# Ten V slots, wq tails that share partitions, softmax sums in place, and new output projection rates

## The chip, the cores and the metric

The kernel runs on one core of a Trainium2 chip. The time is the device time of one execution in microseconds (us); the profile is one execution taken by the hardware profiler. The engines are TensorE (PE; PEld is its weight load), VectorE (DVE), ScalarE (ACT), GpSimd (POOL) and SyncE (SP), which issues nearly all transfers here.

## What is computed

Two independent attention blocks, A and B, with shapes that are the same: 16 batches, 144 query rows of width 448, 16 heads of width 256, 512 cached keys, all in bf16. The two outputs are set side by side.

```python
def _A_ref(x, k_cache, v_cache, wq, wo):          # _B_ref is the same, with rep = 1
    B, Sq, D = x.shape                            # 16, 144, 448
    H, Dh = 16, 256
    q = (x @ wq).reshape(B, Sq, H, Dh).transpose(0, 2, 1, 3)
    scores = jnp.einsum("bhqd,bhkd->bhqk", q, k_cache) * (Dh ** -0.5)
    p = softmax(scores, axis=-1)
    o = jnp.einsum("bhqk,bhkd->bhqd", p, v_cache)
    return o.transpose(0, 2, 1, 3).reshape(B, Sq, H * Dh) @ wo
```

## The kernel before, in words

A **unit** is one head of one batch: 512 units, A's in 0 to 255, B's in 256 to 511 (the first 32 alternate between batches 0 and 1, the rest go batch by batch). For each unit the kernel makes the query `q` (transposed, from `wq` and `x`), the scores against K (transposed, keys on the partitions), the exponentials, and the product with V; four slices of 128 keys each. The result is scaled by the reciprocal of the row sums and put into `ring`, three chunks of 128 output rows long, from which the output projection takes it. A chunk's projection is 32 pieces (one matrix product of 128 x 448 each, `t_op_piece`, L1335), issued in twos; there are 18 chunks for each block.

**The order of the work** is written out by a loop over steps `i` (L1515 on). Step `i` issues, in this order: transfers whose step has come, a query product for unit i+3 or i+4 with its cast (`t_q`, `t_evac_q`), the scores of unit i+2 or i+3 with their exponentials (`t_s`, L1163 and L1173), the V product of unit i (`t_pv`, L1219), the product that makes the row sums (`t_sum`, L1235), the fold of unit i+2 (`t_halves`, L1197), the two adds of unit i+3 on POOL (`t_presum`, L1183 and L1188), logarithm and reciprocal of the sums on ScalarE (`t_ln`, `t_recip`), two checks of the sums' size (`t_check`), the scaling into `ring` (`t_evac_ot`, L1271), and pieces of the output projection. Each engine executes its list in that order and waits by semaphores; a small bookkeeper (`_Sched`) derives the waits from what each instruction reads and writes, tile by tile.

**The row sums.** POOL adds the exponentials of slices 0, 1 to those of 2, 3 (`pp_sb`), then the two halves of that to each other. From unit 48 on (`P0`) that second add goes to `p2_sb`, and VectorE folds its upper 64 partitions onto the lower ones into half of `ps_sb` (one half for an even unit, one for the odd one after it), so that one matrix product with blocks of ones makes the sums of two units. `ln` goes to `ln_sb`, and two exponentials of 64 partitions each make the reciprocal in one of two slots of `rinv_sb`.

**The queries.** `x` has 448 columns: three slices of 128 and a tail of 64. `wq_sb` holds four slices; in the fourth, partitions 64 to 127 are zero, so that whatever `x`'s fourth slice has there doesn't count. From unit 48 on one query product serves the same head of two neighbouring batches where it can (288 columns in place of 144), every second step.

**Transfers.** A planner in Python (L1414 to L1510) lays all loads in one order for SyncE: each load has a use (a step), a step from which its place is free, and an assumed duration. V comes in pairs of units into a ring of `NV` = 9 slots, in which the first 48 units' K also lies (those are transposed by TensorE); later K comes 16 units at a time by a transposing transfer (`t_load_k`, L1039) into a ring for 32 units. `wq` and `wo` of B take the place of A's while the kernel goes over from A to B.

**The rate of the projection.** `op_schedule` (L1378) gives a credit at each step: `OP_RATE` times 18 x 32 / 256 pieces. Its entries are (up to this unit, rate). Pieces that are ready and have credit go into that step. In the last 30 steps the credit is raised, so that all that is ready goes out.

Of the kernel before, what the change touches and what calls it, by code (L numbers as in the profile page):

```python
# [752 lines left out]
def bass_concat_heads__mha_block_cached__gqa_block_cached__near_ridge_kernel(  # L753
# [41 lines left out]
    NV, NX = 9, 6  # L795
# [7 lines left out]
    NQT, NPT, NPS, NRI, NOST = 11, 4, 2, 2, 2  # L803
# [3 lines left out]
    OP_DELAY, OP_START, OP_RATE = 2, (28, 16), ((240, 1.0), (292, 1.35), (600, 1.15))  # L807
# [5 lines left out]
    NRUN = max(n for n in range(1, 33) if NCK % n == 0)  # L813
# [9 lines left out]
    with contextlib.ExitStack() as es:  # L823
# [8 lines left out]
        wq_sb = sb("wq_sb", [128, 4, H * DH], BF16)  # L832
# [4 lines left out]
        xt_sb = sb("xt_sb", [128, 4, NX, SQ], BF16)  # L837
        qt_sb = sb("qt_sb", [128, NQT, 2, SQ], BF16)
# [3 lines left out]
        ps_sb = sb("ps_sb", [128, NPS, SQ], BF16)  # L842
        rinv_sb = sb("rinv_sb", [128, NRI, SQ], F32)
        p2_sb = sb("p2_sb", [128, SQ], F32)
        ln_sb = sb("ln_sb", [128, SQ], F32)
        run_sb = sb("run_sb", [128, 2, NRUN], BF16)
        runs_sb = sb("runs_sb", [128, 2, NCK // NRUN], F32)
        ost_sb = sb("ost_sb", [128, NOST, D], BF16)
        stat = sb("stat", [128, 4], F32)
        flag_sb = sb("flag_sb", [128, 4], I32)  # L850
# [52 lines left out]
        def t_init():  # L903
# [10 lines left out]
            def e2(v):  # L914
                return v.memset(wq_sb[64:128, 3, :], 0.0)
            S.add(DVE, e2, writes=[("wqz", 0)], name="wqz")
# [21 lines left out]
        def t_load_wq(pr, h0, h1, eng=SP):  # L938
            cols = slice(h0 * DH, h1 * DH)
            w = wqs[pr]  # L940
            sem = "wq%d" % (h0 // 4 if h1 != 1 and h1 != 2 else HG + h0)

            def e(q):
                q.dma_start(wq_sb[:, 0:3, cols], w[0:384, cols].rearrange("(c p) n -> p c n", p=128)).then_inc(
                    sems[sem], 16)
                return q.dma_start(wq_sb[0:64, 3, cols], w[384:448, cols]).then_inc(sems[sem], 16)
            S.add(eng, e, writes=[(("wq", h), pr) for h in range(h0, h1)], dma_sem=sem, n_dma=2,
                  name="wq%d.%d" % (pr, h0))
# [59 lines left out]
        def t_tr_x(g):  # L1008
# [19 lines left out]
            S.add(ACT, e2, reads=[("opp", ("x", g))], writes=[(("xt", g), g)], banks=["op"], name="exa%d" % g)  # L1028

# [90 lines left out]
        def t_q(U):  # L1120
# [5 lines left out]
            def e(t):  # L1126
                ins = None
                for dc in range(2):
                    for kc in range(4):
                        c0 = h * DH + dc * 128  # L1130
                        acc = qp_ps[:, dc, 0:2 * SQ] if n == 2 else qp_ps[:, 0, dc * SQ:(dc + 1) * SQ]
                        ins = t.matmul(acc, lhsT=wq_sb[:, kc, c0:c0 + 128],  # L1132
                                       rhs=xt_sb[:, kc, xo:xe + 1:max(xe - xo, 1), :], start=(kc == 0), stop=(kc == 3))
                return ins
            S.add(PE, e, reads=[(("wq", h), pr), ("wqz", 0)] + [(("xt", g % NX), g) for g in gs],
# [41 lines left out]

        def t_presum(U):
            psl = U % NPT
            sl = U % NPS  # L1180
# [4 lines left out]
            dst, key = (ps_sb[:, sl, :], (("ps", sl), U)) if U < P0 else (p2_sb[:, :], ("p2", U))  # L1185
# [5 lines left out]
        def t_halves(U):  # L1191

            sl = U // 2 % NPS
            p0 = U % 2 * 64

            def e(v):
                return v.tensor_tensor(ps_sb[p0:p0 + 64, sl, :], p2_sb[0:64, :], p2_sb[64:128, :], op=ALU.add)  # L1197

            S.add(DVE, e, reads=[("p2", U)], writes=[(("ps", sl), ("p", U // 2)), ("halves", U)], name="hv%d" % U)
# [26 lines left out]
        def t_sum(U):  # L1226
            ob = U % 2
            if U < P0:
                rhs, keys = ps_sb[:, U % NPS, :], [("ones", 0), (("ps", U % NPS), U)]
            else:  # L1230
                sl = U // 2 % NPS
                rhs, keys = ps_sb[:, sl, :], [("ones", 1), (("ps", sl), ("p", U // 2))]
# [5 lines left out]
        def t_ln(U):  # L1238
            ob = U % 2
            dst, key = (rinv_sb[:, U % NRI, :], (("rinv", U % NRI), (U, 0))) if U < P0 else (ln_sb[:, :], ("ln", U))  # L1240
# [5 lines left out]
        def t_recip(U):  # L1246
# [6 lines left out]
            h0 = U % 2 * 64  # L1253
            for p0 in (0, 64):
                def e(a, p0=p0):
                    return a.activation(rinv_sb[p0:p0 + 64, sl, :], ln_sb[h0:h0 + 64, :], AF.Exp, scale=-1.0)  # L1256
# [395 lines left out]
```

## Time and profile before

| | |
|---|---|
| median of 7 runs | 1047.29 us (1045.80 to 1053.54) |
| profiled execution | 1049.42 us, its span 1047.70 us |
| granted TensorE clock, mean | 0.997 |
| bytes moved by DMA | 294.1 MB, mean 281 GB/s |
| V loads | 256 of 512 KB, median 7.5 to 7.7 us from issue to landing |
| K loads by transposing transfers | 30, median 23.1 us (A) and 25.2 us (B) to landing |

A line of the page's groups reads: line of the kernel, engine, operation, what it writes <- what it reads, shape, count | busy us, mean ns of one | idle time of the engine just before it, and what ended it. In a timeline a line is: start, duration, engine, line, operation; instructions of one kind in a row are merged, and a number in brackets is the engine's idle time before it. A row of windows has the stretch, its length, busy time (and count) of PE, PEld, DVE, ACT and POOL, the granted clock, the DMA share and GB/s. A row of waits has who waited for whom: us in total, times, longest.

### The profile page before, as it was taken

The page shows a single profiled execution, that of the slowest core. Times are in us where ns is not written, and L with a number is a line of the kernel's source. Part 1 is how long each engine was busy: PE and PEld are TensorE (multiplying, and loading weights), DVE is VectorE, ACT ScalarE, POOL GpSimd, SP SyncE. Part 2 cuts the span into 40 slices and gives each one's busy share as a digit, 9 for nine tenths or more (in the row PEclk, how much of TensorE's full clock was granted, in tenths as well). Part 3 has the DMA queues.
Part 4 walks back from the last instruction along what each step waited for, and adds up shares of the span by engine and source line. Part 5 has one row for each costly group of instructions (what it writes and reads, how often), then busy time and mean ns, then how long its engine had stood idle before and what let it go on. Part 6 is the DMA issues. An engine that isn't in the chain of part 4 may idle for free.

```text
span 1047.7 us, 32447 instructions
## 1 busy us (share of the span) xinstructions
PE 1031.8 (98%) x12432; PEld 876.1 (84%) x12432; DVE 742.2 (71%) x2042; ACT 794.3 (76%) x2368; POOL 636.8 (61%) x1030
## 2 busy tenths in 40 slices
PE   8999999999999999999999899999999999999997
PEld 8999888888888888888887788888888888888885
DVE  5776677777677776777776567777776667777775
ACT  5877678778777777778766668787877777788785
POOL 3654556666666666666655556666665656666673
PEclk9999999999999999999999999999999999999999
DMA  9999999999999999999999999999999999999960
GB/s 319 360 347 323 294 277 273 279 275 277 303 280 323 260 266 253 278 305 294 257 284 338 279 280 294 290 282 304 267 282 265 294 265 316 266 276 286 289 216 13
DMA packets 590884, 294.10 MB, mean 281 GB/s; under 512 B 501440, under 2 KB 515904, under 8 KB 590720
## 3 DMA queue, kind: packets, MB, share of 16 engines
q1 hardware_dynamic: 590240, 291.72, 111.7%
q8 instruction: 99, 1.62, 0.6%
q14 instruction: 65, 0.53, 0.1%
q10 hardware_dynamic: 480, 0.23, 0.1%
HBM read 161.74 MB, written 4.13 MB: 158 GB/s over the span
## 4 chain that ended last, share of the span: by engine, by line
PE 93%; DMA 4%; ACT 1%; DVE 1%; SPq 1%; issue 0%; POOL 0%; ACTq 0%; DVEq 0%
PE s_ps L1163 23%; PE qp_ps L1132 23%; PE ot_ps L1219 23%; PE op_ps L1335 19%; DMA kt_sb<-in_B_k_cache_dram 2%; PE ot_ps L1235 2%; PE s_ps L1083 1%; PE qp_ps L1083 1%; PE qp_ps L1335 1%; DMA wq_sb<-in_B_wq_dram 1%; DMA v_sb<-in_B_v_cache_dram 1%; ACT rinv_sb L1256 0%; DMA v_sb<-in_A_k_cache_dram 0%; ACT pt_sb L1173 0%; SPq L1053 0%
## 5 line engine op out<-in xcount | busy, mean ns | idle before, releaser
L1183 POOL TENSOR_TENSOR pp_sb<-pt_sb 128x288 f32<-128x288 bf16 x512 | 385.0, 752 | 314.8 <-ACT pt_sb L1173 299.9
L1173 ACT ACTIVATE pt_sb<-s_ps 128x288 bf16<-128x288 f32 x1024 | 364.5, 408 | 178.8 <-PE s_ps L1163 172.6
L1271 DVE TENSOR_TENSOR ring<-ot_ps,rinv_sb 128x288 bf16<-128x288 f32 (+2 forms) x640 | 242.0, 395 | 149.8 <-ACT rinv_sb L1256 146.3
L1163 PE MATMUL s_ps<-qt_sb,kt_sb 128*128 128x144 bf16 x4096 | 340.6, 226 | 3.8 <-DMA kt_sb<-in_B_k_cache_dram 3.0
L1219 PE MATMUL ot_ps<-pt_sb,v_sb 128*128 128x144 bf16 x4096 | 339.9, 226 | 1.6 <-DMA v_sb<-in_B_v_cache_dram 1.6
L1163 PEld LDWEIGHTS s_ps<-qt_sb,kt_sb 128*128 128x128 bf16 x4096 | 287.3, 98 | 56.8 <-DVE qt_sb L1146 6.4
L1256 ACT ACTIVATE rinv_sb<-ln_sb 64x144 f32<-64x144 f32 x928 | 298.3, 321 | 24.2
L1132 PE MATMUL qp_ps<-xt_sb,wq_sb 128*128 128x288 bf16 (+1 forms) x2368 | 301.1, 270 | 2.7 <-DVE kt_sb L1091 1.5
L1335 PE MATMUL op_ps<-wo_sb,ring 128*128 128x448 bf16 x1120 | 285.6, 353 | 0.0
L1132 PEld LDWEIGHTS qp_ps<-xt_sb,wq_sb 128*128 128x128 bf16 x2368 | 211.1, 98 | 77.9 <-DVE kt_sb L1091 1.6
L1219 PEld LDWEIGHTS ot_ps<-pt_sb,v_sb 128*128 128x128 bf16 x4096 | 274.0, 98 | 2.5 <-DMA v_sb<-in_B_v_cache_dram 1.8
L1188 POOL TENSOR_TENSOR p_sb<-pp_sb 128x144 f32<-128x144 f32 x464 | 227.5, 490 | 75.0 <-DVE ps_sb L1197 10.7
L1286 DVE TENSOR_REDUCE run_sb<-ot_ps 128x1 bf16<-128x144 f32 x560 | 146.6, 304 | 77.4 <-ACT ln_sb L1243 45.0
L1197 DVE TENSOR_TENSOR ps_sb<-p_sb 64x144 bf16<-64x144 f32 x464 | 159.9, 345 | 45.6 <-POOL p_sb L1188 31.7
L1146 DVE CAST qt_sb<-qp_ps 128x576 bf16<-128x576 f32 x216 | 162.1, 750 | 17.2 <-PE qp_ps L1132 14.6
L1335 PEld LDWEIGHTS op_ps<-wo_sb,ring 128*128 128x128 bf16 x1120 | 93.7, 98 | 20.1
L1243 ACT ACTIVATE ln_sb<-ot_ps 128x144 f32<-128x144 f32 x232 | 67.9, 293 | 33.7 <-PE ot_ps L1235 26.9
L1235 PE MATMUL ot_ps<-ps_sb,ones 128*128 128x144 bf16 x280 | 63.3, 226 | 0.0
L1145 DVE CAST qt_sb<-qp_ps 128x288 bf16<-128x288 f32 x80 | 35.9, 449 | 2.0 <-PE qp_ps L1132 1.5
L1091 ACT ACTIVATE kt_sb<-qp_ps 128x512 bf16<-128x512 bf16 x48 | 28.9, 602 | 1.2 <-PE qp_ps L1083 1.2
L1188 POOL TENSOR_TENSOR ps_sb<-pp_sb 128x144 bf16<-128x144 f32 x48 | 23.5, 490 | 6.9 <-PE ot_ps L1235 0.3
L1235 PEld LDWEIGHTS ot_ps<-ps_sb,ones 128*128 128x128 bf16 x280 | 27.4, 98 | 0.0
(37 smaller groups left out, 162.5 us busy)
## 6 DMA issues: line engine op xcount, KB each, us to landing
v_sb<-in_A_v_cache_dram SPq DMA_DIRECT2D x128, 512.0 KB, 7.7
v_sb<-in_B_v_cache_dram SPq DMA_DIRECT2D x128, 512.0 KB, 7.5
v_sb<-in_A_k_cache_dram SPq DMA_DIRECT2D x22, 512.0 KB, 10.0
out_dram<-ost_sb SPq DMA_DIRECT2D x36, 112.0 KB, 6.9
wo_sb<-in_A_wo_dram SPq DMA_DIRECT2D x8, 448.0 KB, 7.9
wo_sb<-in_B_wo_dram SPq DMA_DIRECT2D x8, 448.0 KB, 8.6
wq_sb<-in_B_wq_dram SPq DMA_DIRECT2D x4, 768.0 KB, 10.0
wq_sb<-in_A_wq_dram SPq DMA_DIRECT2D x3, 768.0 KB, 9.3
```

What stands on the lines that cost most here:

```text
L1132: ins = t.matmul(acc, lhsT=wq_sb[:, kc, c0:c0 + 128], rhs=xt_sb[:, kc, xo:xe + 1:max(xe - xo, 1), :], start=(kc == 0), stop=(kc == 3))
L1146: return v.tensor_copy(qt_sb[:, a:b + 1:b - a, :, :], qp_ps[:, :, 0:2 * SQ].rearrange("p e (u q) -> p u e q", u=2))
L1163: ins = t.matmul(s_ps[bank][:, (c % 2) * SQ:(c % 2 + 1) * SQ], lhsT=kt_sb[:, 2 * c + dc, ko:ko + 128], rhs=qt_sb[:, qsl, dc, :], start=(dc ...
L1173: return a.activation(pt_sb[:, psl, 2 * k:2 * k + 2, :].rearrange("p b q -> p (b q)"), s_ps[bank][:, 0:2 * SQ], AF.Exp, scale=DH ** -0.5)
L1183: return g.tensor_tensor(pp_sb[:, :, :], pt_sb[:, psl, 0:2, :], pt_sb[:, psl, 2:4, :], op=ALU.add)
L1188: return g.tensor_tensor(dst, pp_sb[:, 0, :], pp_sb[:, 1, :], op=ALU.add)
L1197: return v.tensor_tensor(ps_sb[p0:p0 + 64, sl, :], p2_sb[0:64, :], p2_sb[64:128, :], op=ALU.add)
L1219: ins = t.matmul(ot_ps[ob][:, dc * SQ:(dc + 1) * SQ], lhsT=v_sb[:, vsl, j, c * DH + dc * 128:c * DH + (dc + 1) * 128], rhs=pt_sb[:, sl, c, ...
L1256: return a.activation(rinv_sb[p0:p0 + 64, sl, :], ln_sb[h0:h0 + 64, :], AF.Exp, scale=-1.0)
L1271: ins = v.tensor_tensor(ring[:, 2 * h:2 * h + 2, r0:r0 + q1 - q0], ot_ps[ob][:, 0:2 * SQ].rearrange("p (c q) -> p c q", c=2)[:, :, q0:q1], ...
L1286: return v.tensor_reduce(run_sb[:, k, j:j + 1], ot_ps[ob][:, 2 * SQ:3 * SQ], axis=AX.X, op=op)
L1335: ins = t.matmul(acc[0:m, 0:D], lhsT=ring[:, c, col0:col0 + m], rhs=wo_sb[:, c, :], start=(c == op_first), stop=(c == op_last))
```

## The change

It does six things.

- **A tenth V slot** (`NV` = 10). The planner's rules stay; with ten slots its answer differs.
- **wq's tail shared by two heads.** `wq_sb` has three slices; the tails (64 rows) lie in `wqt_sb`, the even head's in partitions 0 to 63, the odd head's in 64 to 127. A load of wq then has one transfer for the three slices and two for the tails, in runs of 512 bytes. An even head's fourth product reads `xt_sb`'s fourth slice, an odd one's `xu_sb`. So `x`'s tail has to be copied to partitions 64 to 127 of `xu_sb`, and partitions 64 to 127 of `xt_sb`'s fourth slice have to be zero: `t_tail_x`, on VectorE, a copy and a memset for each batch, two or three steps before the batch's first query. The loads of x are planned for three steps earlier.
- **Sums in place.** `p2_sb` goes: the second add writes `pp_sb`'s first half. `ps_sb` has one slot in place of two; before unit 48 odd units use a part of `ost_sb`.
- **Logarithm in place.** `ln_sb` goes: `ln` is written to the odd unit's reciprocal slot; the reciprocal of the odd unit is made in place.
- **Small stores**: `runs_sb` in bf16, `flag_sb` inside `stat`, the checks' runs 20 long in place of 28.
- **Rates**: 1.04 up to unit 200, 0.85 to 240, 1.4 to 292, then 1.1; before 1.0 to 240, 1.35 to 292, then 1.15.

```diff
-    NV, NX = 9, 6
+    NV, NX = 10, 6
...
-    NQT, NPT, NPS, NRI, NOST = 11, 4, 2, 2, 2
+    NQT, NPT, NRI, NOST = 11, 4, 2, 2
...
-    OP_DELAY, OP_START, OP_RATE = 2, (28, 16), ((240, 1.0), (292, 1.35), (600, 1.15))
+    OP_DELAY, OP_START, OP_RATE = 2, (28, 16), ((200, 1.04), (240, 0.85), (292, 1.4), (600, 1.1))
...
-    NRUN = max(n for n in range(1, 33) if NCK % n == 0)
+    NRUN = max(n for n in range(1, 21) if NCK % n == 0)
...
-        wq_sb = sb("wq_sb", [128, 4, H * DH], BF16)
+        wq_sb = sb("wq_sb", [128, 3, H * DH], BF16)
+        wqt_sb = sb("wqt_sb", [128, H // 2 * DH], BF16)
...
+        xu_sb = sb("xu_sb", [128, NX, SQ], BF16)
...
-        ps_sb = sb("ps_sb", [128, NPS, SQ], BF16)
+        ps_sb = sb("ps_sb", [128, SQ], BF16)
...
-        p2_sb = sb("p2_sb", [128, SQ], F32)
-        ln_sb = sb("ln_sb", [128, SQ], F32)
...
-        runs_sb = sb("runs_sb", [128, 2, NCK // NRUN], F32)
+        runs_sb = sb("runs_sb", [128, 2, NCK // NRUN], BF16)
...
-        stat = sb("stat", [128, 4], F32)
-        flag_sb = sb("flag_sb", [128, 4], I32)
+        stat = sb("stat", [128, 8], F32)
+        flag_sb = stat.bitcast(I32)[:, 4:8]
...
-                return v.memset(wq_sb[64:128, 3, :], 0.0)
-            S.add(DVE, e2, writes=[("wqz", 0)], name="wqz")
+                return v.memset(xu_sb[0:64, :, :], 0.0)
+            S.add(DVE, e2, writes=[("xuz", 0)], name="xuz")
...
+            p0, p1 = h0 // 2, (h1 + 1) // 2
+            tails = [] if h0 % 2 else [0, 1]
+
...
-                q.dma_start(wq_sb[:, 0:3, cols], w[0:384, cols].rearrange("(c p) n -> p c n", p=128)).then_inc(
+                ins = q.dma_start(wq_sb[:, 0:3, cols], w[0:384, cols].rearrange("(c p) n -> p c n", p=128)).then_inc(
...
-                return q.dma_start(wq_sb[0:64, 3, cols], w[384:448, cols]).then_inc(sems[sem], 16)
-            S.add(eng, e, writes=[(("wq", h), pr) for h in range(h0, h1)], dma_sem=sem, n_dma=2,
-                  name="wq%d.%d" % (pr, h0))
+                for k in tails:
+                    src = w[384:448, p0 * 2 * DH:p1 * 2 * DH].rearrange("p (g e n) -> p g e n", e=2, n=DH)[:, :, k, :]
+                    dst = wqt_sb[k * 64:k * 64 + 64, p0 * DH:p1 * DH].rearrange("p (g n) -> p g n", n=DH)
+                    ins = q.dma_start(dst, src).then_inc(sems[sem], 16)
+                return ins
+            S.add(eng, e, writes=[(("wq", h), pr) for h in range(h0, h1)] + [(("wqt", p), pr) for p in range(p0, p1) if tails],
+                  dma_sem=sem, n_dma=1 + len(tails), name="wq%d.%d" % (pr, h0))
...
+        def t_tail_x(g):
+            sl = g % NX
+
+            def e1(v):
+                return v.tensor_copy(xu_sb[64:128, sl, :], xt_sb[0:64, 3, sl, :])
+            S.add(DVE, e1, reads=[(("xt", sl), g)], writes=[(("xu", sl), g)], name="xu%d" % g)
+            if g in X_AT:
+                return
+
+            def e2(v):
+                return v.memset(xt_sb[64:128, 3, sl, :], 0.0)
+            S.add(DVE, e2, reads=[(("xt", sl), g)], writes=[(("xt", sl), g)], name="xz%d" % g)
+
...
-                        ins = t.matmul(acc, lhsT=wq_sb[:, kc, c0:c0 + 128],
-                                       rhs=xt_sb[:, kc, xo:xe + 1:max(xe - xo, 1), :], start=(kc == 0), stop=(kc == 3))
+                        w, x = wq_sb[:, kc, c0:c0 + 128] if kc < 3 else wqt_sb[:, h // 2 * DH + dc * 128:][:, 0:128], xt_sb[:, kc]
+                        if kc == 3 and h % 2:
+                            x = xu_sb
+                        ins = t.matmul(acc, lhsT=w, rhs=x[:, xo:xe + 1:max(xe - xo, 1), :], start=(kc == 0), stop=(kc == 3))
...
-            S.add(PE, e, reads=[(("wq", h), pr), ("wqz", 0)] + [(("xt", g % NX), g) for g in gs],
+            S.add(PE, e, reads=[(("wq", h), pr), (("wqt", h // 2), pr), ("xuz", 0)] + [(("xt", g % NX), g) for g in gs] +
+                  ([(("xu", g % NX), g) for g in gs] if h % 2 else []),
...
+        def ps_natural(U):
+            if U % 2:
+                return ost_sb[:, 1, 0:SQ], (("ost", 1), ("ps", U))
+            return ps_sb[:, :], ("ps", U)
+
...
-            sl = U % NPS
...
-            dst, key = (ps_sb[:, sl, :], (("ps", sl), U)) if U < P0 else (p2_sb[:, :], ("p2", U))
+            dst, key = ps_natural(U) if U < P0 else (pp_sb[:, 0, :], ("pp", ("p2", U)))
...
-            sl = U // 2 % NPS
...
-                return v.tensor_tensor(ps_sb[p0:p0 + 64, sl, :], p2_sb[0:64, :], p2_sb[64:128, :], op=ALU.add)
-
-            S.add(DVE, e, reads=[("p2", U)], writes=[(("ps", sl), ("p", U // 2)), ("halves", U)], name="hv%d" % U)
+                return v.tensor_tensor(ps_sb[p0:p0 + 64, :], pp_sb[0:64, 0, :], pp_sb[64:128, 0, :], op=ALU.add)
+
+            S.add(DVE, e, reads=[("pp", ("p2", U))], writes=[("ps", ("p", U // 2)), ("halves", U)], name="hv%d" % U)
...
-                rhs, keys = ps_sb[:, U % NPS, :], [("ones", 0), (("ps", U % NPS), U)]
+                rhs, key = ps_natural(U)
+                keys = [("ones", 0), key]
...
-                sl = U // 2 % NPS
-                rhs, keys = ps_sb[:, sl, :], [("ones", 1), (("ps", sl), ("p", U // 2))]
+                rhs, keys = ps_sb[:, :], [("ones", 1), ("ps", ("p", U // 2))]
...
-            dst, key = (rinv_sb[:, U % NRI, :], (("rinv", U % NRI), (U, 0))) if U < P0 else (ln_sb[:, :], ("ln", U))
+            sl = U % NRI if U < P0 else NRI - 1
+            dst, key = rinv_sb[:, sl, :], (("rinv", sl), (U, 0))
...
-            h0 = U % 2 * 64
-            for p0 in (0, 64):
-                def e(a, p0=p0):
-                    return a.activation(rinv_sb[p0:p0 + 64, sl, :], ln_sb[h0:h0 + 64, :], AF.Exp, scale=-1.0)
-                S.add(ACT, e, reads=[("ln", U // 2 * 2)], writes=[(("rinv", sl), U)], name="rc%d.%d" % (U, p0))
+            if U % 2 == 0:
+                for p0 in (0, 64):
+                    def e(a, p0=p0):
+                        return a.activation(rinv_sb[p0:p0 + 64, 0, :], rinv_sb[0:64, NRI - 1, :], AF.Exp, scale=-1.0)
+                    S.add(ACT, e, reads=[(("rinv", NRI - 1), (U, 0))], writes=[(("rinv", 0), U)], name="rc%d.%d" % (U, p0))
+                return
+
+            def e(a):
+                a.activation(rinv_sb[0:64, NRI - 1, :], rinv_sb[64:128, NRI - 1, :], AF.Exp, scale=-1.0)
+                return a.activation(rinv_sb[64:128, NRI - 1, :], rinv_sb[64:128, NRI - 1, :], AF.Exp, scale=-1.0)
+            S.add(ACT, e, writes=[(("rinv", NRI - 1), U)], name="rc%d" % U)
...
-                load(first_q[g0], (g1 - NX) * H - lq(NT) if g1 > NX else s_min, 1.3 + 0.55 * (g1 - g0), t_load_x, XG)
+                load(first_q[g0] - 3, (g1 - NX) * H - lq(NT) if g1 > NX else s_min, 1.3 + 0.55 * (g1 - g0), t_load_x, XG)
...
+            for g, at_q in first_q.items():
+                if (-2 + g if g in X_AT else at_q - 2 - g % 2) == i:
+                    t_tail_x(g)
```

## The prediction

> **What bounds the kernel now.** I read the page's first two parts, then the chain that ended last, the waits of TensorE, windows over the stages, SyncE's issues, and timelines of single steps.
>
> ```profile
> PE 1031.8 (98%) x12432; PEld 876.1 (84%) x12432; DVE 742.2 (71%) x2042; ACT 794.3 (76%) x2368; POOL 636.8 (61%) x1030
> ...
> PE 93%; DMA 4%; ACT 1%; DVE 1%; SPq 1%; issue 0%; POOL 0%; ACTq 0%; DVEq 0%
> ```
>
> TensorE is busy for 1031.8 of 1047.7 us and is 93% of the chain. The change takes no matrix product away: a query's fourth slice still has 128 rows, half of them zeros on one side. So it can only win back TensorE's waits, or add some.
>
> ```profile
> PE s_ps L1163 <- DMA kt_sb<-in_B_k_cache_dram: 3.0, 1, 3.0
> PE ot_ps L1219 <- DMA v_sb<-in_B_v_cache_dram: 1.6, 1, 1.6
> PE qp_ps L1132 <- DVE kt_sb L1091: 1.5, 1, 1.5
> ...
> PE qp_ps L1132 <- DMA wq_sb<-in_B_wq_dram: 0.9, 1, 0.9
> ```
>
> Three of these lie at the passage from problem A to B: at 521.5 us (wq of B), 561.6 (V) and 600.5 (K). Together 5.5 us, and the last also costs clock:
>
> ```profile
> 601.75:605.20 3.45, 3.45 (x22) 2.60 (x20) 1.52 (x3) 1.12 (x4) 1.15 (x2) 0.51 1.04 387
> 605.20:608.00 2.80, 2.80 (x33) 2.20 (x31) 1.46 (x6) 2.31 (x8) 1.63 (x3) 1.00 1.07 405
> ```
>
> The third number from the right is the granted clock: about half for 3.4 us, so some 1.7 us lost. The passage holds 5.5 + 1.7 = **7.2 us** that a better order of transfers could win. The other side is how closely the softmax sums run, seen in the last units (start, duration):
>
> ```profile
> 1022.67 0.30 DVE L1197 TENSOR_TENSOR ps_sb<-p_sb 64x144 bf16<-64x144 f32 x1
> 1022.78 0.79 POOL L1183 TENSOR_TENSOR pp_sb<-pt_sb 128x288 f32<-128x288 bf16 x1
> ...
> 1024.03 0.45 DVE L1145 CAST qt_sb<-qp_ps 128x288 bf16<-128x288 f32 x1
> 1024.49 0.73 POOL L1183 TENSOR_TENSOR pp_sb<-pt_sb 128x288 f32<-128x288 bf16 x1 [0.29 <-ACT pt_sb L1173]
> 1024.51 0.88 DVE L1197 TENSOR_TENSOR ps_sb<-p_sb 64x144 bf16<-64x144 f32 x1
> 1024.63 0.66 PE L1163 MATMUL s_ps<-qt_sb,kt_sb 128*128 128x144 bf16 x8
> 1025.47 0.49 POOL L1188 TENSOR_TENSOR p_sb<-pp_sb 128x144 f32<-128x144 f32 x1 [0.24 <-DVE ps_sb L1197]
> ```
>
> POOL's first add (L1183) now starts while VectorE still folds the unit before it (L1197). And the query cast ends at 1024.48, 0.15 us before the scores that read it: VectorE has almost no room here.
>
> **The sums in place.** The second add now writes into `pp_sb`, so the first add of the next unit must wait for the fold (before, only the second add waited, for `p2_sb`). Behind it on POOL stands the second add; VectorE's next fold waits for that, and behind the fold stand the two checks, the output scaling and the next query cast. The loop of two units: 0.79 + 0.14 (gap between the adds in the timeline) + 0.49 + 0.05 (POOL to VectorE) + 0.30 + 0.08 (back) = 1.85, and with 0.73 for the other unit 1.79; **3.64 us a pair**. The fold's 0.88 beside an add falls away, since they no longer overlap.
>
> TensorE's pair is longer in the body: the sums' products (L1235) at 701.86 and 705.66 are 3.80 apart. There the loop fits with 0.16 over; the fold comes some 0.3 later, and the 0.2 to 0.6 for which VectorE now waits for the reciprocal take that. Cost nothing; without that cover 0.1 to 0.3 a pair. In the last pairs these products start at 1005.36, 1008.90, 1012.22, 1015.54, 1018.99, 1022.31, 1025.63, 1028.95 and 1032.27: eight pairs in 26.91 us, while the loop wants 8 x 3.64 = 29.12. Nothing behind covers it, since the fold's lateness reaches the cast, the cast the scores. **+2.2 us**.
>
> Here the Trainium skill speaks otherwise. Its page "SBUF — State Buffer", section "Who interferes with whom", says that a VectorE instruction with two SBUF inputs and a GpSimd instruction that reads SBUF shut each other out. Then the new wait orders what could not overlap, and costs only its signal. The row shows less: the add that began 0.19 before the fold's end (1022.78) took 0.79 against 0.73, so it lost 0.06 and not 0.19. With full exclusion the first 0.79 holds 0.60 of work: 3.45 a pair, 8 x 0.13 = 1.0 us. I take the row's 2.2.
>
> The same close pairs stand at units 234 to 250, where the new rate 0.85 takes another two pieces away (2.94 instead of 3.32 us in one pair): a lag of up to 1.6, some 0.7 at TensorE. It goes into the waits at 521 and 561, which are set by transfers. Cost 0; without that cover 0.7. `ln` written into the odd reciprocal slot now waits for the scaling of the odd unit; it already ends 0.05 to 0.1 before `ln` starts in the tightest pairs. The single `ps_sb` makes the fold wait for the sum's product, which the check behind it awaits anyway. Both 0, at most 0.5.
>
> **The tenth V slot and the rates.** A rate of 1.0 is 18 x 32 / 256 = 2.25 pieces a unit, 0.19 us each (two in 0.38). By unit 200 the new rate has done 14 more, by 237 4, by 268 6, by 285 2, by 300 none (counted from the rule). TensorE's work is moved, not changed. What sets the end of the passage is the transfer queue:
>
> ```profile
> 491.72 23.23 SPq L1039 DMA_TRANSPOSE kt_sb<-in_B_k_cache_dram  x1
> ...
> 530.16 25.63 SPq L1039 DMA_TRANSPOSE kt_sb<-in_B_k_cache_dram  x1
> ...
> 576.03 22.21 SPq L1039 DMA_TRANSPOSE kt_sb<-in_B_k_cache_dram  x1
> ```
>
> The third of these feeds the product at 600.45. Its slots were free at unit 269 (about 565 us), but it was issued some ten later, behind 10 V and 8 wo loads. V loads issued between 514 and 542 us took 12.5 to land (median; 7.5 over the run), so the engines have a backlog. A slot more lets one V load (512 KB, landings 1.35 apart) go ahead of the K load two before these, but the same loads then stand in the queue up to the third. By the planner's rule the order between the first and the third stays, but for wo loads exchanged with V. So K lands when it did, at most 1 us earlier from idle moments filled. TensorE arrives 2 x 0.19 = 0.4 later, with 0.4 less left: **-0.4**. The longer cover of V (561.6) only makes the wait at 600.5 longer.
>
> Behind it x of B (2.7 of issue) and two V (0.5 each) now go ahead of the next K, which lands some 5 late of 7.3 to spare (landing 627.5, use 634.8): 0.
>
> **The wq tails.** In place of one load of 64 partitions, two of 64 partitions in runs of 512 bytes; the same bytes. Before:
>
> ```profile
> 519.50:521.00 1.50, 1.11 (x6) 0.39 (x4) 1.44 (x4) 0.94 (x3) 0.98 (x3) 1.00 1.04 205
> 521.50:523.00 1.50, 1.47 (x16) 1.30 (x17) 0.29 (x1) 0.04 (x1) 0.00 (x0) 1.00 1.05 388
> ```
>
> The last number is GB/s: beside a tail 205, beside V alone 388. Whether two halves together fill the ports no row shows. That would win back up to 0.7 x 4 = 2.8 us in the queue. The same page, section "Can I just issue two DMAs to hit both halves?", says that they do not. Against it stand the short runs: in the trace's packets 512 bytes take 27 ns, 2 KB 84 (medians), so 4 x 27 - 84 = 24 ns x 256 / 16 = 0.4 us over B's loads, and four issues more of 0.5 on SyncE, hidden in its backlog (2.0 if they aren't). By the packets **+0.4**, by the page's rule on halves no gain: I take both; range -2.8 to +2.4.
>
> **VectorE's tail copies.** 32 copies and 30 memsets of 64 x 144: between 0.06 (the memset L905) and 0.38 (the copy L1023, 128 x 432) each; I take 0.15, nearer to the memset. 9 us in 305 idle; the wait for x comes two or three units before its first use, and x is fetched three units earlier. Most stand in pairs without a query cast, which gives 0.75 free: **+0.3**; bounds -0 and +3. At the start the 1.76 memset of wq shrinks, on nobody's path (VectorE waits until 5.17), and wq's half loads may move the landing at 23.5 by a little: **+0.1** (-0.5 to +0.7).
>
> **Sum**: 2.2 - 0.4 + 0.4 + 0.3 + 0.1 = +2.6. The profiled execution took 1049.42 (span 1047.70 and 1.72 around): 1052.0 there. It is 2.13 above the median of 1047.29, so for the median **1049.9**.
>
> **Rivals.** (a) The passage gains: tails fill both halves and the slot's lead survives, so that about 5 of the 7.2 us go, with the same end: 1044.9. For it: 205 GB/s beside a tail, and the clock lost only after a long wait. Against: the same bytes ahead of the K load. (b) As (a), and the new wait is free by the rule of exclusion, so nothing is lost at the end: about 1041.5. (c) Slower: the loop outgrows the body. Place: the fold behind the cast in pairs of 3.80 us. It decides from 0.16 us more per pair, for instance when the second add finds VectorE's scaling in the port (at 1005.84 POOL waited 0.44 for it). At 0.05 beyond, over some 190 pairs, +9.5: about 1057. Against: such waits are 6.1 us in the whole run, 14 times. (d) The slot does nothing and the close loop is real: my forecast.
>
> **Numbers.** 0.3% of 1047.3 is 3.1 us, about what a measurement can tell here. (d) 0.55, own range 1048 to 1052, 0.30 within 0.3% and 0.25 slower; (a) 0.18, of it 0.06 faster and 0.12 same; (b) 0.10, 0.09 faster and 0.01 same; (c) 0.17 slower. Faster 0.15, same 0.43, slower 0.42. Range 1043.5 to 1054.5: it leaves out most of (b) and half of (c).
>
> **What would show it.** Right: L1183's releaser becomes the fold; no fold of 0.88; L1235 in the last eight pairs about 3.6 apart; the waits for K and V of B still 4 to 6 us in all, with the half clock behind. Wrong: pairs stay at 3.3 at the end (exclusion holds); the wait at 600 falls under 1 us (the queue gained); pairs in the body grow beyond 3.85, or scores wait for casts in all of it.

## The result, and the profile after

The changed kernel takes 1054.55 us (median of 14 runs), the kernel before 1047.55 beside it (35 runs). The ratio is 1.006, 95% interval 1.0045 to 1.0075: some 6.3 us slower. I had forecast +2.6, that is 1049.9 with a range up to 1054.5; 1.006 times the 1047.29 of the forecast is 1053.6, inside the range near its upper end, and the median itself lies 0.05 beyond. One of the 14 runs took 1178.99 at a granted clock of 0.85, a slow state, and is left out of the ratio. A second measurement of the same kernel (the first experiment) gave 1.0059. The profiled execution of the first took 1051.93 (span 1050.2), 2.6 under the median; that of the second 1056.81 (span 1055.0). They are read together, since one of them alone tells too little, as will be seen.

The profile's page of the changed kernel, the engines and the chain that ended last:

```profile
PE 1034.1 (98%) x12432; PEld 875.2 (83%) x12432; DVE 721.3 (69%) x2112; ACT 794.6 (76%) x2368; POOL 625.4 (60%) x1030
...
PE 88%; DMA 4%; DVE 4%; POOL 2%; ACT 1%; issue 1%; SPq 0%; DVEq 0%; POOLq 0%; ACTq 0%
...
L1210 POOL TENSOR_TENSOR pp_sb<-pt_sb 128x288 f32<-128x288 bf16 x512 | 373.9, 730 | 367.7 <-DVE ps_sb L1223 159.6
...
L1223 DVE TENSOR_TENSOR ps_sb<-pp_sb 64x144 bf16<-64x144 f32 x464 | 141.4, 305 | 150.0 <-POOL pp_sb L1215 93.7
```

TensorE has as many products as before. VectorE and POOL now stand in the chain with 6% (1% before): POOL's first add (L1210, the old L1183) waits for the fold (L1223), and the fold for POOL's second add (L1215). That is the new loop. The fold's mean is 305 ns in place of 345: none of 464 is over 0.31 us, where 30 before were over 0.6.

The waits of TensorE in the same execution:

```profile
PE s_ps L1186 <- DMA kt_sb<-in_B_k_cache_dram: 2.5, 1, 2.5
PE s_ps L1186 <- DVE qt_sb L1169: 1.1, 3, 0.5
PE ot_ps L1245 <- DMA v_sb<-in_B_v_cache_dram: 1.1, 1, 1.1
```

The K wait at 600 us is there (2.5, before 3.0), with the clock behind it at 0.55 in this row of windows (third number from the right):

```profile
598.60:602.40 3.80, 3.68 (x23) 2.77 (x24) 0.46 (x1) 1.46 (x4) 1.21 (x2) 0.55 1.04 386
```

The waits for wq at 521 and V at 561 are gone, and the V wait of 1.1 is a new one, at 754 us.

**Where the time went.** For each unit I take the start of its V product (L1245, before L1219), subtract that of the profile before, and subtract 0.19 us for each projection piece by which the rates have moved work ahead of that unit (counted from the rule). What is left is time lost or won up to there. It is flat nearly everywhere, with steps at a few places. Each number is the step of one execution, in us against the one profile of before; "sum" is all of the run, small steps elsewhere included.

| profile | units 0-8 | 200-248 | 248-280 | 280-312 | 344-376 | 488-511 | sum |
|---|---|---|---|---|---|---|---|
| changed | -1.0 | +1.6 | -2.5 | -0.1 | +1.1 | +2.1 | +2.0 |
| e1 changed, again | +0.1 | +1.6 | -2.5 | -1.6 | +6.3 | +2.1 | +7.1 |
| e2 before, sums in place | +1.0 | +0.4 | -2.9 | -3.3 | +1.8 | +2.1 | -0.4 |
| e3 before, tails | -0.9 | +0.3 | -2.9 | -0.5 | +0.1 | 0.0 | +1.6 |
| e4 changed, x late | -1.0 | +1.5 | -2.5 | +2.6 | +0.7 | +2.1 | +4.2 |
| e5 changed, own store at the end | +1.0 | +1.6 | -2.5 | -0.3 | +4.2 | -0.1 | +4.2 |
| e6 changed, own store | +1.1 | +0.9 | -2.5 | +0.3 | +4.2 | 0.0 | +4.8 |
| e7 changed, nine slots | -1.1 | +1.6 | -2.5 | -0.6 | +1.4 | +2.1 | +1.4 |
| e8 before, new rates | -0.9 | +0.8 | -2.5 | +0.6 | +0.7 | 0.0 | -2.5 |
| e9 changed, one x load late | -1.0 | +1.6 | -0.5 | +0.6 | +1.8 | +2.1 | +6.7 |
| e10 as e9, own store at the end | -0.9 | +1.5 | -0.3 | +2.2 | +0.3 | -0.1 | +5.5 |
| e11 as e10, old rates | +1.2 | +0.6 | -0.4 | -1.9 | +3.3 | -0.1 | +4.7 |
| e12 before, x early | +1.1 | 0.0 | -2.9 | -0.3 | +0.2 | 0.0 | +2.7 |

Two columns repeat to a tenth in all kernels that share a part, whatever else an execution does: the end, and units 200 to 248. Those in which a load can be late (280-312, 344-376) spread by several us for one and the same kernel: changed and e1 are the same program. And the -2.5 to -2.9 in 248-280 is no gain of the change. It stands in e2, e3, e8 and e12 as well, kernels before with one part changed. The waits for wq (0.9) and V (1.6) that the prediction counted into the passage are in none of the profiles e1 to e8, all taken on one chip, nor in the first of the changed kernel; they come again in e9 to e11, on another chip. So they come and go without the change. I take an execution without them for the usual one of before, some 2.5 under that profile, which fits its time of 2.13 above the median; then the two profiles of the changed kernel are some 4.5 and 9.6 above the usual one, with a mean of 7.0 beside the 6.3 measured.

### The profile page after: what moved, and what is told of

It reads as the page before. It is cut to its first block, busy times and chain, and to the rows that moved or that the text cites. A ratio compares the mean times of both kernels' runs of the same rounds, so it can differ in the third digit from the quotient of the medians.

```text
span 1050.2 us, 32294 instructions
## 1 busy us (share of the span) xinstructions
PE 1034.1 (98%) x12432; PEld 875.2 (83%) x12432; DVE 721.3 (69%) x2112; ACT 794.6 (76%) x2368; POOL 625.4 (60%) x1030
## 4 chain that ended last, share of the span: by engine, by line
PE 88%; DMA 4%; DVE 4%; POOL 2%; ACT 1%; issue 1%; SPq 0%; DVEq 0%; POOLq 0%; ACTq 0%
PE qp_ps L1155 22%; PE s_ps L1186 22%; PE ot_ps L1245 22%; PE op_ps L1368 18%; DMA kt_sb<-in_B_k_cache_dram 2%; PE ot_ps L1261 2%; POOL pp_sb L1210 1%; PE s_ps L1103 1%; PE qp_ps L1103 1%; DVE ring L1304 1%; DVE ps_sb L1223 1%; DVE run_sb L1319 1%; POOL pp_sb L1215 1%; ACT rinv_sb L1283 1%; DVE qt_sb L1169 1%
## 5 line engine op out<-in xcount | busy, mean ns | idle before, releaser
L1210 POOL TENSOR_TENSOR pp_sb<-pt_sb 128x288 f32<-128x288 bf16 x512 | 373.9, 730 | 367.7 <-DVE ps_sb L1223 159.6
L1245 PE MATMUL ot_ps<-pt_sb,v_sb 128*128 128x144 bf16 x4096 | 340.2, 226 | 1.2 <-DMA v_sb<-in_B_v_cache_dram 1.1
L1245 PEld LDWEIGHTS ot_ps<-pt_sb,v_sb 128*128 128x128 bf16 x4096 | 274.3, 98 | 2.1 <-DVE ring L1304 1.3
L1155 PE MATMUL qp_ps<-xt_sb,wq_sb 128*128 128x288 bf16 (+1 forms) x1776 | 268.7, 270 | 0.8 <-ACT xt_sb L1034 0.5
L1215 POOL TENSOR_TENSOR pp_sb<-pp_sb 128x144 f32<-128x144 f32 x464 | 227.3, 490 | 36.4
L1223 DVE TENSOR_TENSOR ps_sb<-pp_sb 64x144 bf16<-64x144 f32 x464 | 141.4, 305 | 150.0 <-POOL pp_sb L1215 93.7
L1155 PEld LDWEIGHTS qp_ps<-xt_sb,wq_sb 128*128 128x128 bf16 x1776 | 161.1, 98 | 65.9 <-DVE qt_sb L1169 2.3
L1283 ACT ACTIVATE rinv_sb<-rinv_sb 64x144 f32<-64x144 f32 x464 | 149.5, 322 | 13.0
L1270 ACT ACTIVATE rinv_sb<-ot_ps 128x144 f32<-128x144 f32 x280 | 82.6, 295 | 34.7 <-PE ot_ps L1261 28.7
L1155 PE MATMUL qp_ps<-xu_sb,wqt_sb 128*128 128x288 bf16 (+1 forms) x304 | 81.2, 267 | 0.0
L1288 ACT ACTIVATE rinv_sb<-rinv_sb 64x144 f32<-64x144 f32 x232 | 74.5, 321 | 5.7
L1155 PE MATMUL qp_ps<-xt_sb,wqt_sb 128*128 128x288 bf16 (+1 forms) x288 | 78.5, 273 | 0.0
L1289 ACT ACTIVATE rinv_sb<-rinv_sb 64x144 f32<-64x144 f32 x232 | 74.1, 319 | 2.7
L1261 PE MATMUL ot_ps<-ps_sb,ones 128*128 128x144 bf16 x256 | 57.9, 226 | 0.0
```

What stands on the lines that cost most here:

```text
L1155: ins = t.matmul(acc, lhsT=w, rhs=x[:, xo:xe + 1:max(xe - xo, 1), :], start=(kc == 0), stop=(kc == 3))
L1210: return g.tensor_tensor(pp_sb[:, :, :], pt_sb[:, psl, 0:2, :], pt_sb[:, psl, 2:4, :], op=ALU.add)
L1215: return g.tensor_tensor(dst, pp_sb[:, 0, :], pp_sb[:, 1, :], op=ALU.add)
L1223: return v.tensor_tensor(ps_sb[p0:p0 + 64, :], pp_sb[0:64, 0, :], pp_sb[64:128, 0, :], op=ALU.add)
L1245: ins = t.matmul(ot_ps[ob][:, dc * SQ:(dc + 1) * SQ], lhsT=v_sb[:, vsl, j, c * DH + dc * 128:c * DH + (dc + 1) * 128], rhs=pt_sb[:, sl, c, ...
L1283: return a.activation(rinv_sb[p0:p0 + 64, 0, :], rinv_sb[0:64, NRI - 1, :], AF.Exp, scale=-1.0)
```

## The experiments

Two theories. **Loop**: the new wait of POOL for the fold costs 2 to 3 us where units come closely, above all at the end. **Transfers**: the loss lies in late V and K loads, since the order of the loads on SyncE has changed. Each run was timed in five rounds beside the kernel before. The first four (e1 to e4) and the next four (e5 to e8) ran on one chip, e9 to e12 on another, where the kernel before took 1051.0 (median of 24).

### e1: the changed kernel again

No edit.

> The changed kernel once more, nothing edited, to see by a second profile what its runs above 1054 us have that its first profiled run (1051.9) did not. Theory S (the sums' loop costs about 2.2 us in the last units, the rest of the loss is transfers that come late): ratio 1.004 to 1.008; products of the sums in the last eight pairs about 3.6 us apart as in the first profile; if this profile is of a run above 1054, its extra time lies in waits for K or V, not in the last units. Theory Q (all of the loss is in the transfer queue): the same ratio, and the last units differ between fast and slow profiles.

Measured: 1.0059 (1.0041 to 1.0076), median 1055.91. The table's first two rows show in what its executions differ: in the steps for loads, 5.2 of it at units 344 to 376. There TensorE waited 3.45 us for V, and then ran at half clock:

```profile
756.85 1.12 PE L1245 MATMUL ot_ps<-pt_sb,v_sb 128*128 128x144 bf16 x8 [3.45 <-DMA v_sb<-in_B_v_cache_dram]
```

```profile
756.85:760.50 3.65, 3.65 (x19) 2.51 (x20) 1.29 (x4) 0.94 (x3) 1.22 (x2) 0.50 1.05 402
760.50:764.00 3.50, 3.50 (x36) 3.16 (x34) 1.52 (x3) 2.01 (x6) 1.22 (x2) 0.68 1.06 394
```

Clock 0.50 for 3.65 us and 0.68 for 3.5: 1.8 + 1.1 = 2.9 lost behind the wait, and 3.45 + 2.9 is the step of 6.3. In the first profile the same V load came 1.1 late and the clock stayed at 1.00, a step of 1.1.

### e2 and e3: one part at a time on the kernel before

e2 has the sums and logarithm in place (no `p2_sb`, no `ln_sb`, one slot of `ps_sb`) and nothing else:

```diff
-            dst, key = (ps_sb[:, sl, :], (("ps", sl), U)) if U < P0 else (p2_sb[:, :], ("p2", U))
+            dst, key = ps_natural(U) if U < P0 else (pp_sb[:, 0, :], ("pp", ("p2", U)))
```

e3 has the shared tails of wq, VectorE's copies and the earlier x loads:

```diff
-        wq_sb = sb("wq_sb", [128, 4, H * DH], BF16)
+        wq_sb = sb("wq_sb", [128, 3, H * DH], BF16)
+        wqt_sb = sb("wqt_sb", [128, H // 2 * DH], BF16)
+        xu_sb = sb("xu_sb", [128, NX, SQ], BF16)
...
-                load(first_q[g0], (g1 - NX) * H - lq(NT) if g1 > NX else s_min, 1.3 + 0.55 * (g1 - g0), t_load_x, XG)
+                load(first_q[g0] - 3, (g1 - NX) * H - lq(NT) if g1 > NX else s_min, 1.3 + 0.55 * (g1 - g0), t_load_x, XG)
```

> The kernel before with the sums and the logarithm in place alone (nine V slots, old wq layout, old rates). Theory S: slower by 2.0 to 3.0 us (ratio 1.002 to 1.003), all of it after unit 490, the waits for K and V of B as before. Theory Q: no change (within 1 us). If the new wait delays the body too: 5 us or more.

> The kernel before with the shared wq tails alone (two transfers for the tails, the copies on VectorE, the loads of x planned three steps earlier; nine V slots). Theory S: wq of B lands 1 to 3 us earlier, so the waits at the passage shrink by 1 to 2 us, and the earlier x makes V or K late by 1 to 3 us elsewhere: together -1 to +2 us. Theory Q: this part carries the loss, +4 to +7 us.

Measured: e2 1.0032 (1.0015 to 1.0049), some 3.4 us; e3 1.0008 (0.9993 to 1.0023). The end's +2.1 comes with the sums in place and not with the tails, and e2 has another 0.4 at units 200 to 248. The rest of e2's loss lies in the spread of its loads: its profile, with 1049.38 the fourth fastest of 22 runs, happened to miss the K wait altogether. e3 lost nothing at the end, but 4.2 us between units 104 and 168: two V waits, 3.6 in all, behind a K load that an x load had been put ahead of (x issued at 270.23 for 8.94 us, K at 279.22; in the profile before K at 273.42, x behind it at 292.04). In e12, with the same order of loads, x took 4.60 there and nothing was lost.

### e4: x loads planned as before

```diff
-                load(first_q[g0] - 3, (g1 - NX) * H - lq(NT) if g1 > NX else s_min, 1.3 + 0.55 * (g1 - g0), t_load_x, XG)
+                load(first_q[g0], (g1 - NX) * H - lq(NT) if g1 > NX else s_min, 1.3 + 0.55 * (g1 - g0), t_load_x, XG)
```

> The changed kernel with the loads of x planned for their first query, as before, not three steps ahead of it; all else as changed. Theory S: the wait for V at 754 us (1.1 us in the first profile) goes and K of unit 304 lands earlier, so 1 to 4 us faster than the changed kernel (ratio to before 1.002 to 1.005), unless VectorE's copy then waits for x. Theory Q: 4 us or more faster than the changed kernel. If the place of x's loads does not matter: ratio as the changed kernel's, 1.006.

Measured: 1.004 (1.0026 to 1.0053), about 2 us under the control e1, with intervals that overlap. The step at 344-376 is 0.7 here, but V came 2.3 late at some 632 us, behind a K load of 23.1 us, and cost 4.1. So the place of the loss moved; loads are late by a little at several places, and which of them shows differs by execution.

### e5 and e6: the second add gets its own store again

In e5 from unit 488 on, over x slots that are done by then; in e6 in the whole run, with the first add's result in bf16 to make room.

```diff
+        P2END = 488
+        p2_end = xt_sb[:, 0, 2:4, :].rearrange("p a n -> p (a n)").bitcast(F32)
...
             dst, key = ps_natural(U) if U < P0 else (pp_sb[:, 0, :], ("pp", ("p2", U)))
+            keys = [key]
+            if U >= P2END:
+                dst, keys = p2_end, [(("xt", 2), ("p2", U)), (("xt", 3), ("p2", U))]
```

> The changed kernel, but from unit 488 on POOL's second add writes to a place of its own (f32, over the x slots of batches 26 and 27, which are done by then), so that the next unit's first add no longer waits for the fold. Loop theory: the last eight pairs take 26.9 us again in place of 29.1, about 2.1 us less between units 488 and 508, and the ratio to the kernel before goes from 1.006 to about 1.004. Transfer theory (the loss lies in late V and K loads, the end is only where it becomes visible): the last pairs keep 29 us or the time is given back behind them, and the ratio stays at 1.006.

> The changed kernel with a separate store for the second add in the whole run; to make room the first add's result is held in bf16. Loop theory: as with the store at the end alone, 2.1 us at the end, and 0.4 to 0.8 at units 234 to 250 as well: ratio about 1.003; folds of 0.88 us come back. Transfer theory: ratio 1.006. If the ratio is under that of the run with the store at the end alone by more than 1 us, the wait also costs in the body.

Measured: both 1.0039 (1.0023 to 1.0056; 1.0020 to 1.0058), 2 us under the changed kernel, with intervals that overlap. In the trace the end's step falls from +2.1 to -0.1 and 0.0. In e6 the step at units 200 to 248 falls from 1.6 to 0.9, the rates' part alone (e8: 0.8), so there too the wait cost some 0.6 (0.4 in e2, with the old rates). The timeline of the changed kernel's end (start, duration, engine, line):

```profile
1023.01 0.73 POOL L1210 TENSOR_TENSOR pp_sb<-pt_sb 128x288 f32<-128x288 bf16 x1 [0.48 <-DVE ps_sb L1223]
...
1023.32 0.23 PE L1261 MATMUL ot_ps<-ps_sb,ones 128*128 128x144 bf16 x1
...
1023.82 0.49 POOL L1215 TENSOR_TENSOR pp_sb<-pp_sb 128x144 f32<-128x144 f32 x1
...
1024.42 0.30 DVE L1223 TENSOR_TENSOR ps_sb<-pp_sb 64x144 bf16<-64x144 f32 x1 [1.06 <-PE qp_ps L1155]
1024.86 0.73 POOL L1210 TENSOR_TENSOR pp_sb<-pt_sb 128x288 f32<-128x288 bf16 x1 [0.55 <-DVE ps_sb L1223]
1025.44 0.44 DVE L1168 CAST qt_sb<-qp_ps 128x288 bf16<-128x288 f32 x1
...
1026.65 0.73 POOL L1210 TENSOR_TENSOR pp_sb<-pt_sb 128x288 f32<-128x288 bf16 x1 [0.48 <-DVE ps_sb L1223]
...
1026.95 0.23 PE L1261 MATMUL ot_ps<-ps_sb,ones 128*128 128x144 bf16 x1
```

From one first add to the next 1.85 and then 1.79: 3.64 a pair, and the sums' products (L1261) follow 3.63 apart. The same products in e5, and its fold:

```profile
1022.17 0.82 DVE L1230 TENSOR_TENSOR ps_sb<-xt_sb 64x144 bf16<-64x144 f32 x1
...
1023.20 0.23 PE L1269 MATMUL ot_ps<-ps_sb,ones 128*128 128x144 bf16 x1
...
1025.40 0.88 DVE L1230 TENSOR_TENSOR ps_sb<-xt_sb 64x144 bf16<-64x144 f32 x1
...
1026.52 0.23 PE L1269 MATMUL ot_ps<-ps_sb,ones 128*128 128x144 bf16 x1
```

3.32 apart, although the fold takes 0.82 to 0.88 again in every second unit. A fold slowed beside an add is cheaper here than an add that waits for the fold.

### e7 and e8: the slot and the rates

```diff
-    NV, NX = 10, 6
+    NV, NX = 9, 6
```

```diff
-    OP_DELAY, OP_START, OP_RATE = 2, (28, 16), ((240, 1.0), (292, 1.35), (600, 1.15))
+    OP_DELAY, OP_START, OP_RATE = 2, (28, 16), ((200, 1.04), (240, 0.85), (292, 1.4), (600, 1.1))
```

The first is on the changed kernel, the second on the kernel before.

> The changed kernel with nine V slots, all else as changed. If the tenth slot does nothing (my forecast): ratio 1.006 as with ten. If the slot gives the loads a lead that the rest of the change eats up: 1.008 or more, with V waits of over 2 us at units 280 to 304. If the slot lets V loads go ahead of the transposing K loads and makes those late: under 1.004.

> The kernel before with the new projection rates alone (nine slots, own store for the second add). If rates only move work: 1.000, within 1 us. If the sparse stretch of units 200 to 240 makes the sums and casts run too closely even without the loop, or TensorE reaches the passage too early: 1.001 to 1.003, with the loss at units 200 to 310 in the trace. If they help the passage: under 0.999.

Measured: e7 1.0047 (1.0027 to 1.0067), e8 1.0008 (0.9995 to 1.0021). Nine slots are not slower than ten in the changed kernel: no gain of the slot is to be seen, and a small loss (1.3 us between the centres) is inside the interval. The rates alone cost 0.8 at units 200 to 248, where fewer pieces lie between the units; the ratio can't tell that from nothing.

### e9 to e12: the order of one x load, and what adds up

The table puts the widest step of the changed kernel at units 344 to 376. SyncE's issues there, first in the changed kernel, then in e8, which has the order of before:

```profile
721.02 9.46 SPq L988 DMA_TRANSPOSE xt_sb<-in_B_x_dram  x1
730.53 0.58 SPq L1073 DMA_DIRECT2D v_sb<-in_B_v_cache_dram  x1
731.15 19.15 SPq L1059 DMA_TRANSPOSE kt_sb<-in_B_k_cache_dram  x1
750.35 2.71 SPq L1073 DMA_DIRECT2D v_sb<-in_B_v_cache_dram  x5
```

```profile
723.20 20.47 SPq L1039 DMA_TRANSPOSE kt_sb<-in_B_k_cache_dram  x1
743.72 0.58 SPq L1053 DMA_DIRECT2D v_sb<-in_B_v_cache_dram  x1
744.34 4.09 SPq L981 DMA_TRANSPOSE xt_sb<-in_B_x_dram  x1
748.47 2.12 SPq L1053 DMA_DIRECT2D v_sb<-in_B_v_cache_dram  x4
```

A transposing load holds SyncE for as long as its row says, and nothing else is issued in that time. Ahead of the K load, x pushes that back from 723.20 to 731.15, and the V loads behind it to 750.35. The first of these landed at 754.33 and was used at 754.47, after the wait of 1.10. e9 plans this x load (the seventh group of batches) and the last one as before; that puts this one behind its K load again; by the planner's rule all loads ahead of it keep their order:

```diff
-                load(first_q[g0] - 3, (g1 - NX) * H - lq(NT) if g1 > NX else s_min, 1.3 + 0.55 * (g1 - g0), t_load_x, XG)
+                load(first_q[g0] - (3 if XG < 6 else 0), (g1 - NX) * H - lq(NT) if g1 > NX else s_min, 1.3 + 0.55 * (g1 - g0), t_load_x, XG)
```

e10 is e9 with e5's store at the end, e11 is e10 with the rates of before, and e12 is the kernel before with x planned three steps earlier and nothing else.

> The changed kernel with one move in the order of transfers: the load of x for batches 24 to 27 goes behind the transposing K load that it now precedes (where it stands in the kernel before); the x loads ahead of it stay early. x theory: V loads behind that K load are issued about 8 us sooner, the loss at units 360 to 368 (1.2 to 6.4 us in five profiles of kernels with the early order) goes, and the ratio to before falls from 1.006 to about 1.003. Loop theory alone (all of the loss is the sums' loop): ratio stays at 1.006, and the V wait at some 754 us was there in one or the other profile only.

> The same move, and the second add with its own store from unit 488 on, as in the earlier run. If both causes add up: 2.1 us less again, ratio about 1.001; no step at units 360 to 368 and none at 488 to 508. If the end only waits for transfers, as with the move alone.

> The same two repairs with the projection rates of before. If the sparse stretch of units 200 to 240 costs 0.4 to 0.8 us where the sums run in place: ratio 1.000 to 1.0005, about 0.6 us under the run with the new rates. If the old rates make TensorE reach K at 600 us sooner: the wait there grows by 0.4 and nothing is won.

> The kernel before with x planned three steps earlier and nothing else. x theory: x goes ahead of a K load in five of eight places, V or K waits of 1 to 4 us appear behind one of them (units 136 to 152, 290 to 310 or 360 to 368): ratio 1.001 to 1.003. If early x costs only beside the other changes: 1.000.

Measured: e9 1.0044 (1.0029 to 1.0059), e10 1.0018 (1.0008 to 1.0029), e11 1.0067 (1.0041 to 1.0093), e12 1.0067 (1.0042 to 1.0092).

- e10 against e9, on one chip: 2.7 us less, of which the trace shows 2.2 at the end (+2.1 to -0.1). The loop's price stands, and its repair is worth about what the trace says, though the intervals of the two ratios touch at 1.0029.
- e9 is 1.6 us under the changed kernel, where 3 were expected. The intervals overlap, and the changed kernel itself was not run on this second chip. In the step at 344-376, the five profiles with x, one V load and then K (changed, e1, e5, e6, e7) have 1.1, 6.3, 4.2, 4.2 and 1.4 (mean 3.4); the seven with x behind K have 0 (before), 1.8 (e2), 0.7 (e4), 0.7 (e8), 1.8 (e9), 0.3 (e10) and 3.3 (e11), mean 1.2. So the order costs about 2 us there, and not all of the lateness; as the steps within one group spread as widely, this is argued and not shown.
- The early x is not enough for that step. e3 and e12 have x ahead of this K load too, and lost 0.1 and 0.2 there. They have two V loads between x and K, where the changed kernel has one; here e12, whose K was issued 2.0 later than in the changed kernel:

```profile
722.60 9.38 SPq L981 DMA_TRANSPOSE xt_sb<-in_B_x_dram  x1
732.02 1.09 SPq L1053 DMA_DIRECT2D v_sb<-in_B_v_cache_dram  x2
733.16 20.20 SPq L1039 DMA_TRANSPOSE kt_sb<-in_B_k_cache_dram  x1
```

- By the planner's rule it is the new rates that leave the second V load behind K: e12 with the new rates has the order of e7. So x's earlier place and the rates make this loss together.
- e12 says that x three steps early is slower by itself, by 4 to 10 us on this chip. x passes a K load in three places (at some 271, 600 and 722 us), not in five as I had expected. The profile, the fastest of its six runs, has a K wait of 2.0 at the passage's second K load and V waits of 1.3 and 1.7 later. e3, with the same order of loads on the other chip, lost 0.8 (-0.7 to 2.4). These two don't agree. Whether the split tails win back what early x costs, or the second chip's transfers are slower (three of its four profiles wait for wq and V at the passage, none of the eight on the other chip does; but these three have the split tails, and e12 has not), was not told apart.
- e11 goes against its expectation: with the old rates 5 us are lost, not 0.6 won. By the planner's rule they also change the order of loads around the passage's second K load, and its profile has V waits of 3.1 in the stretch where e10 has 0.3. That does not explain the 5 us: e11's profile (1054.45) is faster than e10's (1055.54, the slowest of its 18 runs). Where they go stays open.

No version tried was faster than the kernel before.

## Why the prediction was right and wrong

**The sums' loop at the end: right.** The forecast was +2.2 and 29.12 us for the last eight pairs. Measured +2.1 in all six profiles with the loop there, 0 within 0.1 in the seven without; eight pairs take 34.22 less 5.17, 29.05. By parts: the add is 0.73, not 0.79, since it no longer starts beside a fold, and the gap between the adds 0.08, not 0.14; but the way back from VectorE to POOL takes 0.14 in place of 0.08, and from POOL to VectorE 0.11 in place of 0.05. The Trainium skill's page "SBUF — State Buffer", section "Who interferes with whom", had given 1.0 (0.7, had I set its 3.45 against the mean pair of 3.36, as I did with my own 3.64): if the two shut each other out, the add that began beside the fold held 0.60 of work. Placed behind the fold it takes 0.73. The row was the better guide.

**The close units at 234 to 250: the step failed.** I saw the place and its price of 0.7, and set the cost to 0, because the waits at 521 and 561 would take it up. None of the profiles e1 to e8 has these waits, so there was no such cover. The loop and the sparse rates together lost 1.6 there in each profile of the changed kernel (0.8 to 0.9 the rates, 0.6 to 0.7 the loop). Whether the K wait at 600 us gave some of it back is not shown: in the profiles that lost these 1.6, the steps at 280-312 go from -1.6 to +2.6.

**The passage: right on K, wrong on what was to be won.** TensorE waited for K at 600 us nearly as long as before, 2.5, with 3.8 us at clock 0.55 behind it, against "-0.4". K was used 1.7 sooner than before (598.72 against 600.45), but in e8, with nine slots, 2.6 sooner (597.88), so that is not the slot's doing. But "waits for K and V of B still 4 to 6 us in all" did not hold in the first profile, with 2.5 + 1.1, and 2.5 of the 7.2 us were waits that come and go from one execution or chip to another. What was to be won was therefore read too large, from one execution that had lost 2.5 us which the changed kernel did not lose, and the change had no part in that.

**x ahead of the next K load: the step that failed most.** "K lands some 5 late of 7.3 to spare: 0" had the lateness right and the spare wrong. x held SyncE for 6.5 us and not for 2.7, and K was issued at 608.89 (before 602.13):

```profile
599.68 6.52 SPq L988 DMA_TRANSPOSE xt_sb<-in_B_x_dram  x1
606.25 0.58 SPq L1397 DMA_DIRECT2D out_dram<-ost_sb  x1
606.87 1.97 SPq L1073 DMA_DIRECT2D v_sb<-in_B_v_cache_dram  x3
608.89 19.32 SPq L1059 DMA_TRANSPOSE kt_sb<-in_B_k_cache_dram  x1
```

It landed at 631.77, 4.3 later than before. But its use came at 632.6, 2.2 sooner than before, since the waits at 521 and 561 were gone. Of the 7.3 only 0.8 were left, and in other executions nothing: K waits of 1.3 in e1 and e11 and 2.0 in e12. And the same exchange stands a second time, at 721 us, where I had not looked: 9.5 us of issue, V behind K, and 1.1 to 6.3 lost. I had written down that x is fetched three units earlier, and used it only to show that VectorE's copies find their data.

**wq's tails: no verdict on the two halves.** The rate in the stretch from 517 to 532 us was 371, 343, 372, 350, 355 and 355 GB/s with split tails and ten or nine slots, 322 in e3, and 315 (before), 349 (e2) and 370 (e8) with the single tail. On the second chip it was 330, 319 and 315 with split tails (e9 to e11, which wait for wq) and 369 with the single one (e12, which does not). They overlap, and no run here contradicts what the Trainium skill's page "SBUF — State Buffer", section "Can I just issue two DMAs to hit both halves?", says: that two transfers do not hit both.

**VectorE's copies: their time about right, their price too small.**

```profile
L1041 DVE COPY xu_sb<-xt_sb 64x144 bf16<-64x144 bf16 x32 | 7.3, 229 | 1.0
L1047 DVE MEMSET xt_sb<- 64x72 uint32 x30 | 3.5, 118 | 0.0
```

10.8 us in place of 9. What they cost TensorE is between the steps of e3 in stretches with no late load, 1.5 in all (0.29, 0.18, 0.25, 0.25 and 0.53 in units 8-104, 168-200, 200-248, 312-344 and 432-488). In the changed kernel the same stretches without 200-248 make 1.2 beside e8, which has its rates, and some 0.5 beside the kernel before, since the rates win a little there. I had 0.3. **The start** moved by -1.1 to +1.2 from one profile to the next, with kernels that leave it alone among both ends.

**Sum, beside a usual execution of before:** loop at the end 2.1, units 200 to 248 1.6, copies 0.5 (with what the rates win taken off), and the step at 344-376 3.4 in the mean of the five profiles less 0.7 (e4, e8) to 1.2 (the mean) for the old order: 6.4 to 6.9, where the clock says 6.3. That it comes so close is partly luck: the 3.4 is a mean of steps from 1.1 to 6.3, and the stretch at 280-312, which spreads as widely, is left out. Rivals (a) and (b) needed a passage that gains through the slot; e7 speaks against it. (The 1041.5 of (b) does not follow from its terms either: 1044.9 less the 2.2 of the end is 1042.7.) Rival (c) needed the loop to outgrow the body: between units 376 and 488 the changed kernel lost 0.1 to 0.2. It is the forecast's case (d), but beyond the 1048 to 1052 that I gave it, with a term left at zero that was worth some 2 us, and another that was worth 1.6. That 1053.6 still lies in the whole range is owed to the range's width and not to the sum.

## What to carry to other kernels

Before an edit is costed at nothing because a wait will absorb it, ask whether that wait is there in other executions; when the profile is slower than the median, some of its waits are probably not. When a load is planned earlier, walk the whole issue list and at each place ask what now stands behind it on the queue, above all where a long issue follows; other parts of the change, here the rates, can decide which load that is. A buffer that is saved by writing in place turns a cover into a loop: add up the loop once, and compare it with the shortest pair anywhere in the kernel, not with the usual one.

## What the runs showed of the hardware

- **A late load costs its wait, and from some 2 us on mostly half the clock behind it.** V waits of 1.1, 1.3 and 1.7 came with steps of 1.1, 1.4 and 1.8. Of the 18 waits for K or V of 2.0 us and more in the fourteen profiles, 13 were followed by a granted clock of 0.5, for 3.4 us, or 6.8 in e1 (3.45 at V) and e10 (3.7 at K). Half of 3.4 is 1.7, and waits of 2.5 (e5, e6) came with steps of 4.2. The shortest of the 13 was 2.0 (e7). Behind five the clock stayed at 1.00: 2.0 and 2.2 in e12, 2.1 in e11, 2.3 in e3 and 3.0 in e4. The Trainium skill's page "TensorE: Matmul & The Clock Gate", section "Part 1: The HAM clock gate (the "warmup" mystery)", puts the fall at an idle window of some 3.4 us; at 600 us a wait of 2.5 was followed by clock 0.55, so in this kernel less can be enough.
- **The same x load holds SyncE for 9.2 to 9.5 us or for 3.6 to 4.9**: the long time in six profiles in which it follows seven V loads directly and stands ahead of K, the short one in seven with it behind the K load's 18 to 23 us of issue. In e3, some 3 us after the V loads, it took 5.0. So an earlier place in the list also made it dearer.
- **VectorE's fold took 0.82 to 0.88 in place of 0.30 when POOL's add had begun just before it**, whereas an add that began in the fold's last 0.19 us took 0.79 in place of 0.73, and so lost only 0.06.
